# Order of the last token tiles and of the weight splits in a fused window attention and mixture-of-experts kernel

## The chip, the core and the metric

One core of one Trainium2 chip runs the whole kernel. The metric is the device time of one execution in microseconds (us). The engines named below: TensorE (PE, with PEld for its weight loads), VectorE (DVE), ScalarE (ACT), GpSimd (POOL) and SyncE (SP, which issues most of the transfers).

## What is computed

First a causal attention with a window of 64 positions (8 batches, 8 heads, 576 positions, head size 64), all in float32; then a mixture of experts with one expert per token, over the 4608 rows of 512 that the attention gives.

```python
scores = scale * np.matmul(q, k.transpose(0, 1, 3, 2))       # masked to 0 <= rel < 64
attn = softmax(scores)                                       # over the last axis
x = matmul(attn, v).transpose(0, 2, 1, 3).reshape(4608, 512)
do_compute = x @ w_skip > 0
logits = x[do_compute] @ w_gate                              # 8 experts
e_idx, gate_w = argmax(logits), softmax(logits)[e_idx]
h = np.maximum(xc[mask] @ w1[e], 0.0)                        # 512 -> 1024, per expert e
y[mask] = gate_w[mask, None] * (h @ w2[e])                   # 1024 -> 512
out = x.copy(); out[do_compute] = xc + y
```

## The kernel before, in words

**Attention.** The tokens come in 36 tiles of 128 (NT = 36). A loop over t = 0 to 34 is a software pipeline written out by hand: iteration t issues the scores of tile t + 1, the transposes of the finished rows x of an older tile (`transpose_x`), the transposes of the probabilities of tile t (`transpose_p`), the softmax of tile t + 1 (`soften`: maximum on DVE, then eight exponentials on ACT, four of them at once and four when the returned function `softened` is called), the products with v of tile t - 1 (`tile_out`) and the products of x with the gate weights. From tile 32 on the gate logits are computed tile by tile (`logits`): 16 small products, which write into the bank that the transposes of x used, and a copy of the result (`lg`, ACT). In iterations 33 and 34 `its[0].split` also transposes the rows gathered for the first expert item, casts them on ACT (`xh`) and subtracts on DVE (`xl`).

**Order.** Each engine works through its instructions in the order of the program text, within `tc.manual_schedule()`; between engines only semaphores hold. So the order in which the helpers are called is the order of each engine's queue.

**Banks.** The transposes of x and of p, the logits by rows, the x of the first item and the products `p1` of the experts all take turns in two PSUM buffers of one tag, "t". The pool "late" (tags g, u, w) takes the place of the score buffers when the loop is over.

**Routing.** `route` is a generator that works out a group of tiles' places in the experts' lists in small steps on DVE (`gmx`, `gd`, `gfi`, `gfm`, `goh`, `gohb`, later `gds`, `gs`, `gdi`), with one exponential on ACT (`gex`) and small sums on PE; it queues the writes into the lists on POOL (L628). `routes(n)` takes n steps of what stands in `late`. The last group, tiles 30 to 35, is put into `late` by `logits(35)`.

**Experts.** The work is ten items (256, 288, 128, 360, 328, 288, 248, 240, 160 and 104 rows), each in four quarters. A step k does the products up of quarter k (`up`: two halves f0 and f1 of twelve products each into `p1`, then `hh` = relu on ACT and `hl` = the rest on DVE, which frees `p1`) and the products down of quarter k - 2 (`down`). float32 is computed as three products of values split in two, so every weight piece (512 KB, 128 x 1024, two for each quarter) is loaded by SP into one of six buffers `raw` and split by `weight_split`: a cast on ACT (`whi`, L809) and a subtraction on DVE (`wlo`, L810). There are 72 pieces, numbered in order of first use: 0, 1, 2 and 4 are the up weights of item 0's quarters, 3, 5, 7 and 9 its down weights, 6, 8, 10, 12 the up weights of item 1, and so on. The split pieces stand in a ring of ten. The load of piece n + 6 waits for the split of piece n.

**Chunks.** `expert_chunks` yields after each half of `up` and of `down` and at the end of a step. `expert_chunk` first orders weight splits (`weights_to`) and then lets the generator run on to its next yield. How far it splits: `now` is what the current step needs, `need` what the next step needs as well; while `late` is not empty at most one more than before; `short` is set for the call after the first half of a quarter of a two-tile item and ahead of a step of one. Behind the loop the calls are mixed with the last tiles in this order: x of tile 33, one weight split, products of tile 34, logits 33, call 1 (item 0, quarter 0, f0), p of tile 35, x of tile 34, call 2 (f1), products of tile 35, logits 34, calls 3 and 4 (end of step 0; quarter 1, f0), x of tile 35, call 5 (quarter 1, f1), logits 35, the first step of the last route. Then, while `late` is not empty, two steps of the route and a call: call 6 (transposes of the first rows of item 1, end of step 1), call 7 (quarter 2, f0), call 8 (f1), calls 9 and 10 (down of quarter 0) and so on. Call 5 falls into a moment at which `late` is empty.

Of the kernel before, what the change touches and what calls it, by code (L numbers as in the profile page):

```python
# [10 lines left out]
F32 = mybir.dt.float32  # L11
# [11 lines left out]
P = 128  # L23
NB = S // 64
NT = N // P
NDC = D // P
# [35 lines left out]
RATE = 1  # L62
# [90 lines left out]
def window_attention_moe(ctx: ExitStack, tc, a, out):  # L153
# [163 lines left out]
    banks = {}  # L317
# [18 lines left out]

    def transpose_x(t):
        x = xns.pop(t)
        px = psum.tile([P, NDC, P], F32, name="px", tag="t", bufs=2)
        for c in range(NDC):  # L340
            tick(2, nc.tensor.transpose(px[:, c], x[:, c * P : (c + 1) * P], ident))  # L341
        s0, n = BATCH.get(t, (SINGLY, 4))
        if t == s0:
            xts[s0] = xs.tile([P, NDC, 4, P], F32, name="xt4", bufs=1)
        xt = xts[s0][:, :, (t - s0) % 4]
        nc.scalar.copy(xt, px)  # L346
        if t >= SINGLY:
            singles[t] = px, xt
        elif t == s0 + n - 1:
            ready.append(s0)  # L350
# [384 lines left out]
    late = []  # L735
# [31 lines left out]
    ring, used = [], {}  # L767
# [308 lines left out]
    with tc.manual_schedule():  # L1076
# [33 lines left out]
        for t in range(NT - 1):  # L1110
            score(t + 1)
            if t >= 3:
                transpose_x(t - LAG[t])
            masks = transpose_p(t)
            columns = logit_columns(t)
            feed(t, 0)
            softened = soften(t + 1)
            pace(1)
            feed(t, 1)
            if t == 1:  # L1120
                load_constants()
            if t == 5:
                nc.gpsimd.tensor_copy(base, cf[:, off["base"]])
            masks()
            columns()
            if t >= 1:
                summed = tile_out(t - 1)
                rows = logit_rows()
                softened()
                if t >= FIRSTX:  # L1130
                    its[0].split(xhl[0], t - FIRSTX, "t")()
                if t - LAG[t] >= SINGLY:
                    logits(t - LAG[t])
                if t == TURN:
                    transpose_x(t - 2)
                rows()
                summed()
            else:
                softened()
                feed(t, 2)  # L1140
                feed(t, 3)
            routes(1 if t < 15 else 2 if t < 20 else 3)
            pace(1 if t >= TWICE or len(paced) > 4 else 0)
# [12 lines left out]
        def expert_chunk():  # L1156
            k = place[0]
            last = len(steps) - 1
            need = max(when[part(min(k + 1, last), 0)], when[part(min(k - 1, last), 1)] if k else 0) + 1
            now = max(when[part(min(k, last), 0)], when[part(k - 2, 1)] if k >= 2 else 0) + 1  # L1160
            if turning[0]:
                turning[0] = False
                weights_to(now)
            elif late:
                weights_to(max(now, min(need, ptr["split"] + 1)) if ptr["use"] else now)
            elif steps[min(k, last)][0] >= len(its) - 2:
                weights_to(now if short[0] else max(now, min(need + 2, ptr["split"] + 1)))
            else:
                eager = 0 if short[0] or gathered[0] < 3 else min(ptr["split"] + RATE, ptr["free"] + min(RING, len(ring)) - 1)
                weights_to(max(need, eager))  # L1170
            place[0], c = next(chunks)

        transpose_x(NT - 3)
        weight_split(ptr["split"])
        ptr["split"] += 1
        summed = tile_out(NT - 2)
        logits(NT - 3)
        summed()
# [289 lines left out]
```

## Time and profile before

| what | us |
|---|---|
| median of 3 runs | 414.01 |
| lowest and highest | 413.55, 416.78 |
| profiled execution | 408.61 |
| its span, first to last instruction | 407.0 |
| mean granted TensorE clock | 0.997 |
| PE, DVE, ACT, POOL busy | 376.0, 270.8, 224.4, 178.2 |

The busy time of PE counts matmuls whose ends are modelled, so that a busy PE is not PE at its peak. In the listings in order of time an idle time in brackets is that of the engine just before the instruction, with what ended it.

### The profile page before, as it was taken

How to read it: one execution, taken by the hardware profiler on the slowest of the kernel's cores; microseconds unless marked ns; L12 is line 12 of the kernel's file. 1: busy time of each engine (PE TensorE's matmuls, PEld its weight loads, DVE VectorE, ACT ScalarE, POOL GpSimd, SP SyncE). 2: the span in 40 equal slices, each digit the busy share in tenths (PEclk: the TensorE clock that was granted, in tenths of full speed). 3: DMA queues.
4: the chain of work that ended last, by engine and by line, in shares of the span. 5: the costliest groups of instructions: out<-in, count | busy, mean ns of one | idle time of the engine just before them, and what ended most of it. 6: DMA issues, size and time to landing. Idle time of an engine off the chain costs nothing. (4 is left out here: it accounts for less than half of the span.)

```text
span 407.0 us, 13642 instructions
## 1 busy us (share of the span) xinstructions
PE 376.0 (92%) x5425; PEld 318.1 (78%) x5425; DVE 270.8 (67%) x552; ACT 224.4 (55%) x643; POOL 178.2 (44%) x222
## 2 busy tenths in 40 slices
PE   4879898989889997999999999999999999999993
PEld 3667787767676866898788898888889889888872
DVE  2667778868688856797616789764555566764591
ACT  3767787767667865564315646334425344452670
POOL 5545445467767583475262718116106423010121
PEclk9999999999999999999999999999999999999998
DMA  8988889869877798668738866657657776685460
GB/s 271 321 278 272 284 266 316 299 216 289 279 241 215 220 340 294 200 202 297 275 115 276 263 194 204 209 174 235 217 161 249 262 238 188 207 250 174 156 230 28
DMA packets 40677, 95.68 MB, mean 235 GB/s; under 512 B 7216, under 2 KB 9021, under 8 KB 40604
## 3 DMA queue, kind: packets, MB, share of 16 engines
q1 hardware_dynamic: 33124, 78.21, 59.3%
q0 software_dynamic: 4896, 10.02, 7.5%
q10 hardware_dynamic: 2592, 6.57, 4.8%
q8 instruction: 43, 0.70, 0.7%
q14 instruction: 22, 0.18, 0.1%
HBM read 80.57 MB, written 14.91 MB: 235 GB/s over the span
## 5 line engine op out<-in xcount | busy, mean ns | idle before, releaser
L810 DVE TENSOR_TENSOR wlo<-raw,whi 128x1024 fp32r<-128x1024 f32 x72 | 86.5, 1222 | 24.2 <-ACT whi L809 22.2
L917 ACT ACTIVATE hh<-p 128x256 fp32r<-128x256 f32 (+4 forms) x56 | 22.5, 403 | 94.4 <-PE p L862 91.8
L809 ACT CAST whi<-raw 128x1024 fp32r<-128x1024 f32 x72 | 73.7, 1049 | 0.0
L303 POOL TENSOR_TENSOR ptm<-pm,mask 128x512 f32<-128x512 f32 x36 | 45.9, 1275 | 53.8 <-ACT pm L302 53.6
L860 PE MATMUL p<-x,whi 128*128 128x288 f32 (+5 forms) x224 | 67.4, 301 | 1.8 <-DVE hl L920 1.3
L862 PE MATMUL p<-x,wlo 128*128 128x288 f32 (+5 forms) x224 | 66.0, 295 | 0.6 <-DVE wlo L810 0.6
L861 PE MATMUL p<-x,whi 128*128 128x288 f32 (+5 forms) x224 | 65.8, 294 | 0.0
L285 ACT ACTIVATE s<-ps,nmx 128x64 f32<-128x64 f32 x288 | 62.8, 329 | 1.2
L946 POOL DMA_INDIRECT out<-yo,les x15 | 15.4, 1029 | 95.3 <-DVE yo L945 88.0
L444 PE MATMUL av<-vm,ptm 64*64 64x65 f32 x2048 | 47.4, 223 | 9.2 <-issue 9.1
L920 DVE SCALAR_TENSOR_TENSOR hl<-p,hh 128x256 fp32r<-128x256 f32 (+4 forms) x56 | 24.8, 444 | 46.3 <-ACT hh L917 26.8
L444 PEld LDWEIGHTS av<-vm,ptm 64*64 64x64 f32 x2048 | 39.6, 134 | 16.3 <-issue 14.9
L628 POOL DMA_INDIRECT lists<-ent,gdi x36 | 38.3, 1063 | 19.9 <-issue 12.6
L860 PEld LDWEIGHTS p<-x,whi 128*128 128x128 f32 x224 | 42.2, 188 | 4.7 <-DVE hl L920 1.9
L861 PEld LDWEIGHTS p<-x,whi 128*128 128x128 f32 x224 | 42.2, 188 | 0.9
L862 PEld LDWEIGHTS p<-x,wlo 128*128 128x128 f32 x224 | 42.2, 188 | 0.8 <-DVE wlo L810 0.8
L259 PE MATMUL ps<-k,q 64*64 64x128 f32 (+1 forms) x1024 | 38.5, 274 | 0.9 <-DMA q<-qT 0.4
L276 DVE COPY_PREDICATED ps<-sel,ps 128x512 f32<-128x512 int32 x36 | 24.9, 690 | 18.2 <-PE ps L259 14.0
L346 ACT COPY xt<-px 128x512 f32<-128x512 f32 x36 | 21.2, 589 | 23.8 <-PE px L341 17.6
L259 PEld LDWEIGHTS ps<-k,q 64*64 64x64 f32 x1024 | 31.0, 138 | 4.3 <-issue 2.2
L860 PE MATMUL yv<-whi,hh 128*128 128x512 f32 (+1 forms) x72 | 28.8, 400 | 0.0
L862 PE MATMUL yv<-whi,hl 128*128 128x512 f32 (+1 forms) x72 | 28.2, 392 | 0.0
(188 smaller groups left out, 741.7 us busy)
## 6 DMA issues: line engine op xcount, KB each, us to landing
raw<-wq SPq DMA_DIRECT2D x72, 512.0 KB
vm<-vp SPq DMA_DIRECT2D x32, 260.0 KB
q<-qT SPq DMA_DIRECT2D x32, 256.0 KB
out<-x SPq DMA_DIRECT2D x32, 256.0 KB
k<-kT SPq DMA_DIRECT2D x24, 256.0 KB
w<-wq ACTq DMA_DIRECT2D x12, 512.0 KB
k<-kT SPq DMA_DIRECT2D x8, 384.0 KB
kt<-kT SPq DMA_DIRECT2D x8, 256.0 KB
```

Source lines behind the costliest of these rows:

```text
L259: tick(4, nc.tensor.matmul(ps[64 * hf : 64 * hf + 64, z, p, 64 * w.start :], q[h, p], k[h, w, p], start=True, stop=True, skip_group_check= ...
L276: nc.vector.copy_predicated(cur, sel.unsqueeze(1).unsqueeze(1).to_broadcast([P, 2, 4, 64]), ps[..., :64])
L285: nc.scalar.activation(s[:, q, z], cur[:, z, q], AF.Exp, bias=nmx[:, z, q : q + 1], scale=0.125)
L303: nc.gpsimd.tensor_tensor(part(0, 2), split(pm[:, 0:2], 2), kept(2), op=ALU.mult)
L444: ins = tick(4, nc.tensor.matmul(av[64 * hf : 64 * hf + 64, z, q * VW : (q + 1) * VW], ptm[h, q, 2 * hf + 1 - w], win[hf][w][h, q], start= ...
L628: ins = nc.gpsimd.indirect_dma_start(out=lists, out_offset=bass.IndirectOffsetOnAxis(ap=di, axis=0), in_=ent.bitcast(I32), in_offset=None, ...
L809: nc.scalar.copy(hi, raw)
L810: nc.vector.tensor_tensor(lo, raw, hi.bitcast(F32), op=ALU.subtract)
L860: nc.tensor.matmul(o, lh, rh, start=first, stop=False)
L861: nc.tensor.matmul(o, lh, rl, start=False, stop=False)
L862: nc.tensor.matmul(o, ll, rh, start=False, stop=last)
L920: beat(nc.vector.scalar_tensor_tensor(hl[:, f, :m], p1[:, :m], 0.0, hh[:, f, :m].bitcast(F32), op0=ALU.max, op1=ALU.subtract))
```

## The change

Four edits. In the loop's last iteration, t = 34, the second four exponentials of tile 35 are issued behind the split of the gathered x and the logits of tile 32 instead of ahead of them. Behind the loop the first weight split stands ahead of the transposes and the copy of x of tile 33. The transposes of x of tiles 34 and 35 (and the logits in the same bank) use a bank of their own, tag "u" of the pool "late". And `expert_chunk` orders splits by another rule where `late` is empty and the item is not one of the last two: where `short` is set only what the step needs now, elsewhere at most one more than before (`RATE` is 1), up to the ring or, before three items are gathered, up to `need + 2`.

```diff
     def transpose_x(t):
         x = xns.pop(t)
-        px = psum.tile([P, NDC, P], F32, name="px", tag="t", bufs=2)
+        if t < NT - 2:
+            px = psum.tile([P, NDC, P], F32, name="px", tag="t", bufs=2)
+        else:
+            px = banks["late"].tile([P, NDC, P], F32, name="px", tag="u", bufs=1)
         for c in range(NDC):
...
                 rows = logit_rows()
-                softened()
+                if t < NT - 2:
+                    softened()
                 if t >= FIRSTX:
                     its[0].split(xhl[0], t - FIRSTX, "t")()
                 if t - LAG[t] >= SINGLY:
                     logits(t - LAG[t])
+                if t == NT - 2:
+                    softened()
                 if t == TURN:
                     transpose_x(t - 2)
...
             elif steps[min(k, last)][0] >= len(its) - 2:
                 weights_to(now if short[0] else max(now, min(need + 2, ptr["split"] + 1)))
             else:
-                eager = 0 if short[0] or gathered[0] < 3 else min(ptr["split"] + RATE, ptr["free"] + min(RING, len(ring)) - 1)
-                weights_to(max(need, eager))
+                lead = ptr["free"] + min(RING, len(ring)) - 1 if gathered[0] >= 3 else need + 2
+                weights_to(now if short[0] else max(now, min(lead, ptr["split"] + RATE)))
             place[0], c = next(chunks)
 
-        transpose_x(NT - 3)
         weight_split(ptr["split"])
         ptr["split"] += 1
+        transpose_x(NT - 3)
         summed = tile_out(NT - 2)
```

## Rows read from the trace of the kernel before

**Rows 1.** The page: busy time of PE, and PE in 40 slices (tenths).

```profile
PE 376.0 (92%) x5425; PEld 318.1 (78%) x5425; DVE 270.8 (67%) x552; ACT 224.4 (55%) x643; POOL 178.2 (44%) x222
...
PE   4879898989889997999999999999999999999993
```

**Rows 2.** Table by stretch: length, busy time (instructions) per engine, clock, DMA.

```profile
180.00:200.00 20.00, 18.73 (x115) 16.65 (x114) 16.54 (x34) 11.07 (x20) 9.23 (x9) 1.00 0.79 272
...
240.00:260.00 20.00, 20.00 (x113) 17.95 (x112) 17.47 (x39) 8.93 (x14) 9.47 (x12) 1.00 0.69 223
```

**Rows 3.** Groups by line: the weight split (busy us, mean ns, idle before).

```profile
L810 DVE TENSOR_TENSOR wlo<-raw,whi 128x1024 fp32r<-128x1024 f32 x72 | 86.5, 1222 | 24.2 <-ACT whi L809 22.2 <-issue 1.6
L809 ACT CAST whi<-raw 128x1024 fp32r<-128x1024 f32 x72 | 73.7, 1049 | 0.0
```

**Rows 4.** In order of time, PE, 156 to 174 us (start, us, instruction).

```profile
156.59 0.66 PE L341 MATMUL px<-ident,x 128*128 128x128 f32 x4 [1.05 <-ACT lg L418]
...
158.48 0.64 PE L414 MATMUL px<-wg,xt 128*64 128x9 f32 x16
...
160.12 0.39 PE L862 MATMUL p<-x,wlo 128*128 128x256 f32 x1 [0.57 <-DVE wlo L810]
...
162.52 0.66 PE L341 MATMUL px<-ident,x 128*128 128x128 f32 x4 [0.49 <-DVE hl L920]
...
169.14 0.39 PE L860 MATMUL p<-x,whi 128*128 128x256 f32 x1 [0.49 <-issue]
...
171.79 0.39 PE L860 MATMUL p<-x,whi 128*128 128x256 f32 x1
...
173.34 0.60 PE L849 MATMUL px<-ident,xg 128*128 128x128 f32 x4
```

**Rows 5.** In order of time, ACT, 154 to 174 us.

```profile
154.20 1.75 ACT L285 ACTIVATE s<-ps,nmx 128x64 f32<-128x64 f32 x8
...
157.76 1.05 ACT L809 CAST whi<-raw 128x1024 fp32r<-128x1024 f32 x1
...
169.16 2.00 ACT L809 CAST whi<-raw 128x1024 fp32r<-128x1024 f32 x2
...
173.33 0.25 ACT L505 ACTIVATE gex<-gd 128x48 f32<-128x48 f32 x1 [1.59 <-DVE gd L497]
```

**Rows 6.** In order of time, DVE, 158 to 173 us.

```profile
158.84 1.23 DVE L810 TENSOR_TENSOR wlo<-raw,whi 128x1024 fp32r<-128x1024 f32 x1 [1.70 <-ACT whi L809]
...
172.86 0.19 DVE L495 TENSOR_REDUCE gmx<-lg 128x6 f32<-128x48 f32 x1
```

**Rows 7.** In order of time, PE, 190 to 198 us: products up of item 1.

```profile
190.28 0.29 PE L860 MATMUL p<-x,whi 128*128 128x288 f32 x1
...
192.41 0.40 PE L860 MATMUL p<-x,whi 128*128 128x288 f32 x1 [0.39 <-DVE hl L920]
...
197.88 0.40 PE L860 MATMUL p<-x,whi 128*128 128x288 f32 x1 [0.88 <-DVE hl L920]
```

**Rows 8.** In order of time, DVE and ACT, 179 to 198 us.

```profile
179.63 0.17 DVE L542 TENSOR_REDUCE gdi<-gds 128x6 int32<-128x54 f32 x1
...
188.55 0.38 ACT L917 ACTIVATE hh<-p 128x256 fp32r<-128x256 f32 x1 [3.69 <-PE p L862]
...
191.78 3.90 ACT L809 CAST whi<-raw 128x1024 fp32r<-128x1024 f32 x4
...
192.86 4.63 DVE L810 TENSOR_TENSOR wlo<-raw,whi 128x1024 fp32r<-128x1024 f32 x4 [0.51 <-ACT whi L809]
...
197.41 0.75 DVE L920 SCALAR_TENSOR_TENSOR hl<-p,hh 128x256 fp32r<-128x256 f32 x2
```

**Rows 9.** In order of time, POOL: a list write, and the gather for item 2.

```profile
173.22 0.99 POOL L628 DMA_INDIRECT lists<-ent,gdi  x1 [1.69 <-DVE gmx L495]
...
202.24 1.07 POOL L654 DMA_INDIRECT xg<-out,les  x1 [0.94 <-DMA raw<-wq]
```

**Rows 10.** Table by stretch: behind the last matmul.

```profile
402.00:407.00 5.00, 0.00 (x0) 0.00 (x0) 0.00 (x0) 0.00 (x0) 1.02 (x1) 0.77 0.15 40
```

## What is predicted

> **What bounds the kernel now.** I read the page first: TensorE (PE) is busy for 376.0 of 407.0 us, and its slices show nine tenths or more from about 170 us to the end [rows 1]. The table by stretch then says where time is left: in 180 to 200 us PE lacks 1.27 us of 20, in 240 to 260 nothing [rows 2]. So a change pays only by taking waits off PE between 154 and 206 us, and what PE gains there it keeps, because after it one matmul follows the other to the end. Then I read the three listings in order of time for that stretch, PE first (where does it stand still, and for whom), then ScalarE (ACT) and VectorE (DVE) for the work in front of what it waits for [rows 4 to 8]. In them the reader should see that the waits on PE come from the *order* in ACT and DVE, which work strictly in program order here, and not from how much work they have. One weight split is a cast of 1.05 us on ACT and then a subtraction of 1.22 us on DVE [rows 3], so a matmul that needs a freshly ordered split waits up to 2.3 us. In a row of four, one cast follows the other after 0.95 us and one subtraction after 1.14 us ([rows 8]; (3.90 - 1.05)/3 and (4.63 - 1.22)/3).
>
> **Change 1 to 3: the last token tiles.** In the iteration t = 34 eight exponentials start at 154.20 and take 1.75 us, that is one every 0.197 us; the cast of the gathered x stands behind them, and then the copy of tile 32's logits (`lg`). PE's transposes of x for tile 33 wait 1.05 us for that copy, to 156.59, since they reuse its bank [rows 4]. With four exponentials moved behind, the cast starts at about 155.0, when its transposes are done, and `lg` at 155.62: the transposes start at 155.84, 0.75 earlier. The four exponentials then run from 155.72 (their reader, the transposes of p of tile 35, comes only behind the first chunk's products of 160.12 [rows 4]), so the next ACT work starts at 156.51. It is now the weight split's cast (before: 157.76 [rows 5]); x's copy stands behind it, from 157.46 to 158.05. The logits of tile 33, at 158.48 before [rows 4], wait for that copy and start at 158.08: 0.40 earlier, not 0.75. The rest of the cast's 0.95 us in front of the copy is covered by the products of tile 34, which PE has to do in between anyway.
>
> The subtraction starts at 157.59 instead of 158.84 [rows 6] and ends at 158.82. The first chunk's third matmul, which before waited until 160.12 [rows 4], goes on at about 159.0: 1.1 to 1.2 us earlier. Next the bank: the transposes of x of tile 34 waited 0.49 us for the chunk's `hl` [rows 4]. In a bank of their own they follow the transposes of p at once, and the second chunk's products find a free buffer behind them. That adds 0.6, so the second chunk starts 1.8 us earlier. The same thing at tile 35: there the first products behind the transposes stood still for 0.49 us, at 169.14 [rows 4], for the last chunk's `hl`. So the chunk of 169.14 starts at about 166.8. Sum: **minus 2.35 us**. From below: if the steps behind the first chunk find another wait (GpSimd's masks for tile 35's products), only its 1.2 stays. Nothing can be lost below zero here, since the one thing put in front, the cast, is already charged to the copy. I take 2.35, with 1.2 to 2.4 as bounds: each later gain is a wait that a row shows, with no other due behind it.
>
> **Change 4: one split per chunk.** I counted both rules through all calls of `expert_chunk`. They order the 72 splits alike except in calls 5 to 22. Before: call 5 orders splits 2 and 3; 8 and 9 order 4 and 5; 13 orders 6 and 7; 16 to 22 order 8 to 14, one each. After: 5 none, since the flag `short` is set there and the rule is `now`; 6, 7, 8 and 9 order 2, 3, 4, 5; 11 orders 6; 14 to 21 order 7 to 14; 13 and 22 none. The rows of before agree with the count: two casts in one at 169.16 [rows 5], four in one at 191.78 [rows 8].
>
> *What it costs.* Piece 2 is first used in call 7, by the products that start at 171.79 [rows 4]. Before, its split was done by 171.5. After, call 6 orders it, and ahead of call 6 the program has logits of tile 35, their copy, and the first steps of the last route: `gmx`, `gd` on DVE and the exponential `gex` on ACT, which stood idle 1.59 us for `gd` [rows 5, 6]. So the cast now waits for that chain. Counted from the start T of call 5's products: logits copied at T + 2.47, `gd` at T + 2.75 and `gex` at T + 3.0 (the spacing of `gmx` and `gex`, 0.47 [rows 5, 6]), cast from T + 3.15 to T + 4.20, subtraction from T + 4.23 to T + 5.45. Unhindered the products would start at T + 2.65. They start at T + 4.25, and the third, the first that reads `wlo`, at T + 5.50. Ten more follow at 0.12 us; the transposes that came at 173.34, T + 4.20, [rows 4] now come at T + 6.81. **Plus 2.6 us.** Bounds: 1.6 if only the cast were waited for, and 3.8 if another subtraction of 1.22 [rows 3] got in between. With T = 166.8 that place falls at 173.6, against 173.34: the two parts cancel, to plus 0.25.
>
> *What it moves.* From there both kernels stand alike, but splits 6 and 11 to 14 are ordered one or two calls earlier. Before, PE waited twice for `hl`, which frees the buffer of the products: at 192.41 and at 197.88 [rows 7]. The rows give 0.39 and 0.88 us of idle; with about 0.15 each until the pipeline is full again that is some 1.6 us. The second wait is the row of four: the `hl` at 197.41 stood behind four subtractions that took 4.63 us [rows 8]. Laid end to end in the new order, with the small steps of the expert order in between as before, from 179.85, behind the route's last step [rows 8], DVE does wlo 6 to 181.0, 7 to 185.3, 8 to 187.0, 9 to 188.2, 10 to 189.35, `hl`, 11 to 190.85, `hl`, 12 to 14 to 194.7, and the `hl` that PE needs by 196.5 comes at 195.1. Even if the activations come as late as the one of 188.55 (2.4 us after its last matmul [rows 8], for a reason that the trace doesn't show), it is 196.4. So about 1.4 of the 1.6 us goes: **minus 1.4**, bounds 0 and 1.6.
>
> *Its transfers.* A split issues none itself, but each frees the buffer for the load of the piece six further on, in SP's queue. Loads 8 and 9 start about 1 and 1.4 us later, 12 about 1.9 earlier, 13 one later, 14 as before. No cast stood idle before [rows 3], and casts 8 and 9 come 10 us after their loads begin: I cost it at nothing. Its cover is that lead; for 13 and 14 it is small, and a cast that waits there lands in the bounds above. GpSimd's list writes, held at 173.22 by DVE's `gmx` [rows 9], start some 3.5 us earlier, since no subtraction stands ahead of `gmx` any more; so the gather of the next item's rows at 202.24 [rows 9], which waits for all of them, comes earlier too and will not take the gain back.
>
> **Sum.** Minus 2.35, plus 2.6, minus 1.4: minus 1.15 us. The profiled execution took 408.61 us around a span of 407.0, so I expect 407.45 and 405.85 there. It stands 5.4 us below the median of the runs, 414.01; the difference carried over gives **412.9 us**.
>
> **Rivals.**
> *The fresh split hides.* If ACT or PE did something else in that time, the first part stays whole: minus 2.35, minus 1.4, so 410.3 us. For it: only about 1.6 us of the wait is certain order. Against: the cast stands behind `gex` in an engine that works in order.
> *Nothing is paid back.* If the waits at 192 and 197 hang on the late activations and the loads and not on the row of four, the sum is plus 0.25: 414.3 us. For it: the late activation of 188.55 [rows 8]. Against: four subtractions alone make the second wait.
> *The wait moves in front of the older `hl`* (the slower side). wlo 10 now stands ahead of the `hl` that frees the buffer for the products of 190.28 [rows 7]. That `hl` is due at 189.7 by the order above, the products at 190.5: DVE has 0.85 us to spare. If it runs later than that, each such place costs up to one subtraction, 1.22 us [rows 3], instead of a gain: 414.01 + 0.25 + 1.22 = 415.5 us.
> *The clock falls.* The granted clock was 1.00 (2.4 GHz) in 180 to 200 and 240 to 260 [rows 2] and fell, to a mean of 0.77, behind the last matmul, where PE did nothing any more [rows 10]. If the new stop took it to 1.2 GHz, the 12 matmuls behind it, 1.55 us, would take that again: 412.9 + 1.55 = 414.45 us. The Trainium skill ("TensorE: Matmul & The Clock Gate", section "Why this matters for your kernels") speaks against such stops, and advises against long idle gaps between bursts of matmuls, which drop the clock to half; the trace agrees as far as its end goes. My stop is two pieces of about 1.6 and 1.0 us, with matmuls between.
>
> **How the numbers follow.** Chances: forecast 0.50, split hides 0.16, nothing paid back 0.19, wait moves 0.12, clock 0.03. The range runs from a little under the first rival's 410.3 to a little past the slow one's 415.5: 410.0 to 415.8, which also takes in 3.8 for the stop; what is left out is part of "hides" and some of "moves". One per cent is 4.1 us, about what a measurement here can tell (the three runs lie 3.2 us apart). Under 409.9 only "hides" reaches, with about half its chance and a little from the spread of the runs: 0.10. Over 418.1 none reaches but by several misses: 0.06. Within: 0.84.
>
> **What would show it.** In the profile after: transposes of tile 33 at about 155.8; no wait for `hl` ahead of those of 34 and 35; call 5's products at 166.8. Then, the test of the step that decides, a stop of about 1.6 us for `whi` and one of about 1.0 for `wlo` in the products of piece 2, and the next transposes at 173.6. The four casts in one are gone, and PE waits less than 0.5 us in 190 to 198. If the stop at piece 2 is missing, or is 4 us long, or the waits at 192 and 197 are as before, the matching term was wrong.

## The result and the profile after

| what | before | after |
|---|---|---|
| median of 22 runs each, us | 412.41 | 415.67 |
| lowest and highest, us | 407.86, 416.80 | 411.41, 418.77 |
| profiled execution, us (its span) | 408.61 (407.0) | 416.00 (414.2) |
| mean granted TensorE clock in it | 0.997 | 0.988 |
| PE busy, us | 376.0 | 375.7 |

The ratio of after to before is 1.0073, with an interval of 1.0045 to 1.0102: about 3.0 us slower. That is under 1%, but it is clear of no change, and on the other side than the forecast (1.15 us faster). That the median of after, 415.67, still falls inside the range given (410.0 to 415.8) is luck: the range was laid around 414.01, the median of the first three runs of before. The ratios here leave out executions more than 1.5% above the fastest of their kernel, which the medians keep in, so two variants are compared below by their ratios.

The page of after shows the same work, and a PE that dips where before had nines [rows 1]:

```profile
PE 375.7 (91%) x5425; PEld 319.9 (77%) x5425; DVE 271.5 (66%) x552; ACT 225.0 (54%) x643; POOL 180.6 (44%) x222
...
PE   4879897898989787799989999999999999999993
```

The table by stretch says where PE's time and its clock went (length, busy time and count of PE, PEld, DVE, ACT, POOL, then the clock, the DMA share and GB/s):

```profile
170.00:180.00 10.00, 6.95 (x53) 6.26 (x53) 5.32 (x13) 4.49 (x10) 6.75 (x9) 0.76 0.40 119
...
180.00:200.00 20.00, 20.00 (x129) 18.38 (x128) 17.02 (x42) 12.03 (x20) 10.94 (x8) 0.95 0.75 244
...
200.00:220.00 20.00, 18.42 (x138) 16.17 (x137) 6.82 (x11) 4.43 (x15) 8.32 (x15) 1.00 0.51 176
```

Three microseconds are missing in 170 to 180 us, at a mean clock of 0.76; the records of the granted clock give 1.2 GHz from 175.3 to 182.1 us. The stretch 180 to 200, where before lacked 1.27 us [rows 2], is full. And 1.58 us are missing again in 200 to 220, where before had no wait on PE. PE in order of time shows all three:

```profile
159.72 0.66 PE L344 MATMUL px<-ident,x 128*128 128x128 f32 x4 [1.00 <-ACT lg L421]
...
164.51 0.60 PE L344 MATMUL px<-ident,x 128*128 128x128 f32 x4
...
170.06 0.60 PE L344 MATMUL px<-ident,x 128*128 128x128 f32 x4
170.41 0.36 PE L863 MATMUL p<-x,whi 128*128 128x256 f32 x1
...
172.02 0.64 PE L417 MATMUL px<-wg,xt 128*64 128x9 f32 x16
172.59 0.66 PE L852 MATMUL px<-ident,xg 128*128 128x128 f32 x4
175.79 0.58 PE L863 MATMUL p<-x,whi 128*128 128x256 f32 x1 [2.55 <-ACT whi L812]
...
177.10 0.58 PE L865 MATMUL p<-x,wlo 128*128 128x256 f32 x1 [0.51 <-issue]
177.48 0.41 PE L863 MATMUL p<-x,whi 128*128 128x256 f32 x1
177.69 0.41 PE L864 MATMUL p<-x,whi 128*128 128x256 f32 x1
...
212.72 0.66 PE L852 MATMUL px<-ident,xg 128*128 128x128 f32 x4 [1.58 <-DMA xg<-out,les]
```

The `hl` waits ahead of the transposes of tile 34 and behind those of tile 35 [rows 4] are gone. Piece 2's products wait 2.55 us for `whi`, and from there they come every 0.21 us, not every 0.12. At the first rows of item 2 there is a new wait, for the gather `xg`; before, these transposes started at 205.75 with no wait (shown further below). What stands ahead of piece 2's cast, ACT and then DVE in order of time (with the route's last step `gdi`):

```profile
172.13 0.38 ACT L920 ACTIVATE hh<-p 128x256 fp32r<-128x256 f32 x1 [0.85 <-issue]
173.89 0.17 ACT L421 COPY lg<-px 128x9 f32<-128x9 f32 x1 [1.38 <-PE px L852]
174.56 0.24 ACT L508 ACTIVATE gex<-gd 128x48 f32<-128x48 f32 x1 [0.51 <-DVE gd L500]
174.71 1.03 ACT L812 CAST whi<-raw 128x1024 fp32r<-128x1024 f32 x1
```

```profile
174.09 0.20 DVE L498 TENSOR_REDUCE gmx<-lg 128x6 f32<-128x48 f32 x1 [1.12 <-ACT lg L421]
...
175.78 1.27 DVE L813 TENSOR_TENSOR wlo<-raw,whi 128x1024 fp32r<-128x1024 f32 x1 [0.28 <-ACT whi L812]
...
186.33 0.17 DVE L545 TENSOR_REDUCE gdi<-gds 128x6 int32<-128x54 f32 x1
```

The chain is the one foretold (logits' copy, `gmx`, `gd`, `gex`, cast, subtraction), but the copy came late: 1.23 us behind the last of the logits' products (172.02 + 0.64), with ACT idle. Its row names PE as what ended that wait: in the kept trace the update of PE's semaphore that frees the copy stands at 173.86. So it was PE's release that came late, and not ACT. GpSimd, for the gather (list writes, then the gather of item 2's rows):

```profile
181.21 1.84 POOL L631 DMA_INDIRECT lists<-ent,gdi  x1 [0.30 <-issue]
...
187.26 1.21 POOL L631 DMA_INDIRECT lists<-ent,gdi  x1 [4.21 <-issue]
...
195.01 1.96 POOL L631 DMA_INDIRECT lists<-ent,gdi  x1 [0.30 <-issue]
...
209.21 1.07 POOL L657 DMA_INDIRECT xg<-out,les  x1 [0.94 <-DMA raw<-wq]
```

The last six list writes (187.26 the first, 195.01 the last) wait for the route's last step `gdi`, at 186.33 (179.63 before [rows 8]): GpSimd stands idle 4.21 us ahead of them. The gather comes at 209.21 instead of 202.24 [rows 9]. The same places in before, PE (logits of tile 35, item 2's transposes), ACT (their copy) and GpSimd (first and last of the six writes):

```profile
170.77 0.64 PE L414 MATMUL px<-wg,xt 128*64 128x9 f32 x16
...
205.75 0.66 PE L849 MATMUL px<-ident,xg 128*128 128x128 f32 x4
```

```profile
171.57 0.17 ACT L418 COPY lg<-px 128x9 f32<-128x9 f32 x1
```

```profile
182.31 1.59 POOL L628 DMA_INDIRECT lists<-ent,gdi  x1 [0.30 <-issue]
...
189.78 0.97 POOL L628 DMA_INDIRECT lists<-ent,gdi  x1 [0.30 <-issue]
```

There the six writes came one behind the other after the eight before them, with no wait for `gdi`, and the last stood at 189.78.

**Where the time went.** Executions differ by several microseconds in the attention, so I compare distances from one event to the next: the maximum of tile 35 (ACT `nmx`, 153.96 before), the activations `hh` of call 5 (171.06), of item 0, quarter 3, f0 (180.43), of item 1, quarter 2, f0 (199.76), and the `hh` at 243.21, behind item 2. Each column is the distance less that of before; minus is faster. The last column lists the stretches at 1.2 GHz between 150 and 215 us, by the clock's records of that one execution. Two things limit the comparison. There is one profile of before only, while the sets ran on their own (their medians of before lie between 406 and 413 us), so the columns can hold more than the edit. And in before two casts stand ahead of call 5's `hh`: it starts 1.92 us behind T, the start of call 5's products, and 1.72 behind it in after; counted to T, the last tiles give -1.92 in after and -2.50 in after_here, and the stop 0.2 less, +6.00 and +2.52.

| kernel | last tiles | stop for piece 2 | items 0, 1 | item 2's entrance | sum | 1.2 GHz, us |
|---|---|---|---|---|---|---|
| after | -2.12 | +6.20 | -1.78 | +1.54 | +3.84 | 175.3 to 182.1 |
| after_here | -2.70 | +2.72 | -1.72 | +0.29 | -1.41 | none |
| late2 | -2.85 | +4.11 | -1.78 | -0.52 | -1.04 | 168.8 to 172.3 |
| fill20 | -2.84 | +2.72 | -1.54 | +0.46 | -1.20 | none |
| fill_late2 | -2.32 | +2.72 | -1.78 | -0.82 | -2.20 | none |
| rule_alone | +0.26 | +2.72 | -1.78 | +1.57 | +2.77 | 154.9 to 158.3 |
| call5_two | -0.26 | 0.00 | -0.83 | +3.51 | +2.42 | 157.4 to 160.8, 208.6 to 212.0 |
| call5_late2 | -1.39 | 0.00 | -1.78 | +2.05 | -1.12 | none |
| banks_order | +2.43 | -0.02 | -0.62 | +0.05 | +1.84 | 151.7 to 162.0 |
| banks_late2 | -1.90 | +0.01 | -0.70 | -1.03 | -3.62 | none |
| banks_late2_b | -1.23 | 0.00 | -0.93 | +0.37 | -1.79 | none |
| stop_only | +0.37 | +6.07 | -0.80 | +0.52 | +6.16 | 159.2 to 166.1, 176.3 to 183.1 |
| stop_fill | -1.12 | +3.86 | -1.04 | +1.36 | +3.06 | 159.0 to 162.4 |
| edit1_back | -1.06 | +6.31 | -1.79 | +1.08 | +4.54 | 155.8 to 159.3, 172.9 to 179.7 |
| behind5 | +1.41 | +2.19 | -0.69 | +1.74 | +4.65 | 157.3 to 167.5 |
| behind5_late2 | -2.05 | +2.19 | -1.78 | +1.84 | +0.20 | none |
| ahead_route | -2.20 | +5.54 | -1.79 | +1.46 | +3.01 | 173.9 to 180.7 |

### The profile page after: what moved, and what is told of

Same layout as the page of the kernel before. It is cut to its first block, busy times and chain, and to the rows that moved or that the text cites. A ratio compares the mean times of both kernels' runs of the same rounds, so it can differ in the third digit from the quotient of the medians.

```text
span 414.2 us, 13645 instructions
## 1 busy us (share of the span) xinstructions
PE 375.7 (91%) x5425; PEld 319.9 (77%) x5425; DVE 271.5 (66%) x552; ACT 225.0 (54%) x643; POOL 180.6 (44%) x222
## 5 line engine op out<-in xcount | busy, mean ns | idle before, releaser
L863 PE MATMUL p<-x,whi 128*128 128x288 f32 (+5 forms) x224 | 68.2, 304 | 2.6 <-ACT whi L812 2.5
L865 PE MATMUL p<-x,wlo 128*128 128x288 f32 (+5 forms) x224 | 66.9, 299 | 0.5 <-issue 0.5
L864 PE MATMUL p<-x,whi 128*128 128x288 f32 (+5 forms) x224 | 66.7, 298 | 0.0
L447 PE MATMUL av<-vm,ptm 64*64 64x65 f32 x2048 | 46.5, 223 | 11.7 <-issue 11.7
L631 POOL DMA_INDIRECT lists<-ent,gdi x36 | 39.3, 1092 | 22.4 <-issue 16.0
L863 PEld LDWEIGHTS p<-x,whi 128*128 128x128 f32 x224 | 43.2, 193 | 4.9 <-ACT whi L812 2.8
L864 PEld LDWEIGHTS p<-x,whi 128*128 128x128 f32 x224 | 43.2, 193 | 0.9
L865 PEld LDWEIGHTS p<-x,wlo 128*128 128x128 f32 x224 | 43.1, 193 | 0.8 <-issue 0.8
```

The costliest lines, as they stand in the source:

```text
L447: ins = tick(4, nc.tensor.matmul(av[64 * hf : 64 * hf + 64, z, q * VW : (q + 1) * VW], ptm[h, q, 2 * hf + 1 - w], win[hf][w][h, q], start= ...
L631: ins = nc.gpsimd.indirect_dma_start(out=lists, out_offset=bass.IndirectOffsetOnAxis(ap=di, axis=0), in_=ent.bitcast(I32), in_offset=None, ...
L863: nc.tensor.matmul(o, lh, rh, start=first, stop=False)
L864: nc.tensor.matmul(o, lh, rl, start=False, stop=False)
L865: nc.tensor.matmul(o, ll, rh, start=False, stop=last)
```

## The experiments

Each set has its own runs of the kernel before, with these medians and mean clocks: set 1, 407.87 us and 0.990; set 2, 406.19 and 0.989; set 3, 412.74 and 0.990 (two far outlying executions left out of the clock); set 4, 413.15 and 0.988. Clocks below are means over the executions of a kernel.

### Set 1: the edits apart

**banks_order**: edits 1 to 3 alone, the splits by the old rule.

```diff
-                lead = ptr["free"] + min(RING, len(ring)) - 1 if gathered[0] >= 3 else need + 2
-                weights_to(now if short[0] else max(now, min(lead, ptr["split"] + RATE)))
+                eager = 0 if short[0] or gathered[0] < 3 else min(ptr["split"] + RATE, ptr["free"] + min(RING, len(ring)) - 1)
+                weights_to(max(need, eager))
```

> The changed kernel with the old rule for the splits: only the edits of the last token tiles. Theory A (the loss comes from the new rule: in call 5 no split is ordered, PE stops about 3 us for piece 2, and the clock falls to 1.2 GHz behind the stop): no stop in front of the products of piece 2, one granted clock of 1.00 from 10 us to the last matmul, the products of call 5 about 2 us earlier than before counted from the last iteration, and a time about 2 us below the kernel before, 0.995 of it. Theory B (the bank and the order of the last tiles cost, or the loss is chance in the attention part): no faster than before, 1.000 to 1.007.

406.71 us, ratio 0.9986 (0.9937 to 1.0036), clock 0.988. There is no stop for piece 2. The gain of the last tiles is missing in the profiled execution, whose clock was low in just that place; banks_late2 below shows it.

**rule_alone**: the kernel before with the new rule alone (the same diff the other way round).

> The kernel before with the new rule for the splits alone. Theory A: the stop for piece 2 as in the changed kernel (2.5 us for whi, 0.5 for wlo), the clock at 1.2 GHz for some 7 us behind it, and 5 to 6 us above the kernel before, 1.013 of it, since the gain of the other edits is missing. Theory B: within 0.3 per cent of the kernel before.

409.97 us, ratio 1.0065 (1.0017 to 1.0112), clock 0.986. The rule brings the stop (+2.72), with no low stretch behind it in this execution, gives back 1.78 and loses 1.57 of that at item 2's gather.

**call5_two**: the change, but call 5 orders splits 2 and 3 as before.

```diff
-                weights_to(now if short[0] else max(now, min(lead, ptr["split"] + RATE)))
+                weights_to(need if ptr["split"] == 2 else now if short[0] else max(now, min(lead, ptr["split"] + RATE)))
```

> The changed kernel, but in call 5 the splits 2 and 3 are ordered as before; everywhere else the new rule stands. Theory A: no stop, no fall of the clock, the waits for hl at item 1 gone too, but the gather for item 2 limits: 2 us below the kernel before, 0.995. If the gather does not limit, the waits at item 1 pay as well: 3.5 us below, 0.9915. Theory B: as the changed kernel, 1.005 to 1.01.

409.58 us, ratio 1.0075 (1.0029 to 1.0120), clock 0.985. The stop is gone, the loss is not: so the stop alone is not the cause. PE in order of time, in an execution of 412.87 us, the highest of its twelve:

```profile
207.95 0.66 PE L852 MATMUL px<-ident,xg 128*128 128x128 f32 x4 [2.55 <-DMA xg<-out,les]
...
208.58 0.42 PE L864 MATMUL p<-x,whi 128*128 128x288 f32 x1
208.80 0.44 PE L865 MATMUL p<-x,wlo 128*128 128x288 f32 x1
209.04 0.44 PE L863 MATMUL p<-x,whi 128*128 128x288 f32 x1
```

PE waits 2.55 us for the gather, and then the products come at 0.24 us instead of 0.13: the clock fell behind this wait as it did behind the stop in the profile of after.

**fill20**: the change, with 20 transposes of the identity, used by nothing, between calls 6 and 7.

```diff
             expert_chunk()
+            if fills:
+                fills = 0
+                fl = banks["late"].tile([P, NDC, P], F32, name="fl", tag="w", bufs=2)
+                for c in range(20):
+                    nc.tensor.transpose(fl[:, c % NDC], ident, ident)
```

> The changed kernel with 20 transposes of the identity, into a bank that nothing reads, between call 6 and call 7, that is in PE's stop ahead of piece 2 (about 2.2 us of work, 0.11 us each, more than the kernel needs). If the clock costs beside the wait: the granted clock stays at 1.00, and the time lies some 3 us below the changed kernel, about 1.001 of the kernel before. If only the wait costs: no better than the changed kernel, 1.007, or 0.2 us worse.

406.00 us, ratio 0.9997 (0.9955 to 1.0039), clock 0.991, the highest of the set. The stop is still there (+2.72); with the extra work on PE the change is no slower than before. The change without filler did not run in this set, so what the filler is worth is read from set 3.

### Set 2: the gather of item 2

**after_here**: the change itself.

> The changed kernel itself, beside its variants on one chip, with the granted clock of every execution. Theory C (clock): the work outside the low stretches is as long as before, and what is lost is lost in stretches at 1.2 GHz; so time minus (1 - mean clock) x time lies within 1 us of the same figure of the kernel before (403.6 there in the last set), while the mean clock is 0.004 to 0.008 below it, and the time 2 to 4 us above it. Theory W (waits): the mean clock is the same within 0.002 and the waits for piece 2 and for item 2's rows make the 3 us; then the figure without the clock's loss is itself 2 to 3 us above before.

407.46 us, ratio 1.0048 (1.0006 to 1.0091), clock 0.988 against 0.989. Here neither theory holds as written: the clock is hardly lower, and the time without the clock's loss (402.4 us) lies 0.3 us above before's 402.1. But its profiled execution, at 403.43 us the fastest of its twelve, ran with the clock up and shows the change as it was forecast: -2.70, +2.72, -1.72, +0.29. The stop in it, PE and then ACT in order of time:

```profile
163.86 0.64 PE L417 MATMUL px<-wg,xt 128*64 128x9 f32 x16
...
166.45 0.39 PE L863 MATMUL p<-x,whi 128*128 128x256 f32 x1 [1.37 <-ACT whi L812]
...
167.71 0.39 PE L865 MATMUL p<-x,wlo 128*128 128x256 f32 x1 [0.76 <-DVE wlo L813]
```

```profile
164.55 0.17 ACT L421 COPY lg<-px 128x9 f32<-128x9 f32 x1 [0.20 <-PE px L417]
```

Two pieces, 1.37 and 0.76 us, and the logits' copy on time, where after had 2.55 and a copy 1.2 us late.

**late2**: the change, with item 2's transposes one half of a quarter later.

```diff
-    SPLITS = {1: ((3, 0),), 2: ((2, 1), (3, 0)), 3: ((1, 1), (2, 1), (3, 0))}
+    SPLITS = {1: ((3, 1),), 2: ((2, 1), (3, 0)), 3: ((1, 1), (2, 1), (3, 0))}
```

> The changed kernel, with the transposes of item 2's rows one half of a quarter later. Theory G (the gather limits): the payback of items 0 and 1 was eaten by the wait for that gather, 1.46 us in the profiled execution of the change, 2.4 to 2.6 in others; without it the kernel is 1.5 to 3 us faster than the changed kernel beside it, PE shows no wait ahead of item 2's transposes, and the mean clock rises by 0.001 to 0.003, since one place at which the clock falls is gone. Rival: another wait takes its place (the cast or the subtraction of item 2's rows is then needed at once), and the time is within 0.7 us of the changed kernel.

405.72 us, ratio 1.0014 (0.9974 to 1.0055): 1.4 us under after_here by the ratios, whose intervals overlap; the mean clock did not rise (0.988). The wait is gone from PE:

```profile
203.91 0.66 PE L852 MATMUL px<-ident,xg 128*128 128x128 f32 x4
```

**fill_late2**: both, filler and later transposes.

> The changed kernel with the 20 filler transposes between calls 6 and 7 and with item 2's transposes one half later. Theory C: both places at which PE stands still for 1.5 us or more in the experts' part are covered or gone, so the mean clock is at or above before's (0.990 or more), and the time is 1.5 to 3 us under the kernel before (ratio 0.993 to 0.996). Theory W: the stop for piece 2 is still there, covered only by filler, so the ratio stays at 1.000 to 1.004.

405.78 us, ratio 0.9989 (0.9947 to 1.0030), clock 0.990. The ratio is lower than after_here's, with intervals that overlap; beside late2 the filler added nothing that can be told here.

**banks_late2**: edits 1 to 3 and the later transposes, with the old rule.

> The kernel before with the edits of the last token tiles (no new rule for the splits), and item 2's transposes one half later. banks_order showed a wait of 0.58 us for that gather and a ratio of 0.9986. Theory C: 0.6 us of wait less and perhaps one fall of the clock less: ratio 0.994 to 0.998. Rival (the wait for item 2 is no limit where the old rule holds): the same 0.998 to 1.000.

404.13 us, ratio 1.0003 (0.9961 to 1.0045), clock 0.989: not to be told from before. Its profile keeps 1.90 us of the last tiles.

### Set 3: the stop by itself

**stop_only**: the new rule for splits 2 to 5, the old one from there on.

```diff
+                eager = 0 if short[0] or gathered[0] < 3 else min(ptr["split"] + RATE, lead)
+                if ptr["split"] >= 6:
+                    weights_to(max(need, eager))
+                else:
-                weights_to(now if short[0] else max(now, min(lead, ptr["split"] + RATE)))
+                    weights_to(now if short[0] else max(now, min(lead, ptr["split"] + RATE)))
```

> The changed kernel with the new rule only for splits 2 to 5 and the old one from there on: the stop for piece 2 and the last tiles' edits, without the payback in items 0 and 1. Theory (terms as measured so far): last tiles -2.3 to -2.8, stop +2.7, payback none, gather 0 to +0.5, so -0.3 to +0.6 us while the clock stays up; with a fall of the clock at the stop in about half of the executions (+1.4 to +3.5 in each) +0.5 to +2.2 us on the mean. PE's wait for hl near 192 and 197 is back. Rival (no payback exists, and the stop alone is what the change does): the same time as the changed kernel, and the waits for hl stay away.

416.41 us, ratio 1.0059 (1.0014 to 1.0105), clock 0.981: no execution is above 0.988. One wait for `hl` is back, and of the 1.78 us in items 0 and 1 only 0.80 are left:

```profile
205.54 0.40 PE L863 MATMUL p<-x,whi 128*128 128x288 f32 x1 [0.72 <-DVE hl L923]
```

**stop_fill**: the same with the 20 filler transposes.

> The same as stop_only, with the 20 filler transposes of the identity between calls 6 and 7, which keep PE busy in the wait for piece 2's split and are used by nothing. Theory C (the wait brings falls of the clock with it): no low stretch within 10 us behind the filler, mean clock 0.002 to 0.004 above that of stop_only, and 0.8 to 1.7 us faster than it. Rival (falls come at chance places, the stop has no part in them): the same clock within 0.001 and the same time within 0.5 us.

413.92 us, ratio 1.0038 (1.0005 to 1.0071), clock 0.992. By the ratios 0.9 us faster than stop_only, which the intervals do not settle, with more work on PE and the copy as late; the mean clock is clearly higher (0.992 against 0.981). The table by stretch for both, 170 to 180 us (stop_only, then stop_fill), and then PE in stop_fill:

```profile
170.00:180.00 10.00, 6.94 (x57) 6.25 (x58) 6.40 (x18) 4.25 (x9) 5.74 (x8) 0.82 0.32 90
```

```profile
170.00:180.00 10.00, 8.92 (x86) 8.32 (x85) 6.14 (x16) 5.11 (x10) 6.84 (x7) 1.00 0.37 114
```

```profile
173.60 2.35 PE L1382 MATMUL fl<-ident 128*128 128x128 f32 x20
176.27 0.39 PE L863 MATMUL p<-x,whi 128*128 128x256 f32 x1 [0.32 <-issue]
...
177.53 0.39 PE L865 MATMUL p<-x,wlo 128*128 128x256 f32 x1 [0.76 <-DVE wlo L813]
```

The wait for piece 2 is as long, but filled; the clock stays at 1.00 and the stop costs 3.86 us instead of 6.07. This pair is the plainest evidence here: the wait itself is one price, and the clock that falls with it another, of 2.2 us between these two executions (6.07 less 3.86).

**call5_late2**: call5_two with item 2's transposes later.

> The changed kernel, but call 5 orders splits 2 and 3 as before (no stop for piece 2), and item 2's transposes come one half later (no wait for that gather). Theory G (the stop and the gather wait are what took the gain; the clock adds to it by chance): from the maximum of tile 35 on it keeps the last tiles' 2.3 to 2.8 us and the 1.7 us of items 0 and 1, less what call 5 pays for its two casts (up to 1), so 3 to 4.5 us under the kernel before, ratio 0.989 to 0.994. Rival: call5_two alone was 1.0075, with a mean clock 0.005 below before's; if that comes from falls of the clock in other places than the item-2 wait, this kernel stays at 1.000 or above.

411.58 us, ratio 0.9996 (0.9954 to 1.0038), clock 0.990 like before's, where call5_two stood 0.005 below its own. The clock is back, but the 3 to 4.5 us did not come: the wait for the gather is shorter (0.74 us, 2.55 in call5_two) but not gone, and two other waits at item 2's entrance came to it. PE in order of time, then ACT, first here, then in late2:

```profile
206.62 0.66 PE L852 MATMUL px<-ident,xg 128*128 128x128 f32 x4 [0.74 <-DMA xg<-out,les]
...
215.81 0.44 PE L938 MATMUL pt<-ident,hs 128*128 128x128 f32 x2 [0.42 <-ACT hs L933]
...
218.34 0.66 PE L852 MATMUL px<-ident,xg 128*128 128x128 f32 x4 [0.67 <-DVE hl L940]
```

```profile
211.01 3.23 ACTq L803 DMA_DIRECT2D w<-wq  x2
215.38 0.38 ACT L933 ACTIVATE hs<-p 128x256 f32<-128x256 f32 x1 [7.47 <-remote]
```

```profile
207.94 0.92 ACTq L803 DMA_DIRECT2D w<-wq  x2
209.97 0.38 ACT L933 ACTIVATE hs<-p 128x256 f32<-128x256 f32 x1 [4.79 <-PE p L865]
```

Item 2's first activation `hs` stands in ACT's queue behind two transfers, whose issue spans 3.23 us here and 0.92 in late2. Before had 2.56 at this place, without a wait on PE. What holds the second transfer is not in the trace.

**edit1_back**: the change with the exponentials in front again.

```diff
-                if t < NT - 2:
-                    softened()
+                softened()
...
-                if t == NT - 2:
-                    softened()
```

> The changed kernel with the second four exponentials of tile 35 in front again. By the prediction's step the copy of tile 32's logits then starts 0.75 us later against the maximum of tile 35 (2.41 us behind it as in the kernel before, against 1.62 to 1.77 in undisturbed executions with the edit), and the first chunk's activation about 0.4 to 0.8 us later. Rival (that copy waits for a late release by PE, as in the profiled execution of the change, where it came 2.35 behind): the same distance with and without the edit, and no difference in time.

414.45 us, ratio 1.0057 (1.0015 to 1.0099). The copy of tile 32's logits comes 2.29 us behind the maximum of tile 35; with the edit it is 2.13 to 2.33 in the same set. So in this set the rival holds and the edit moved nothing; in set 2 the same distance was 1.62 to 1.77 in three of four kernels with the edit.

### Set 4: the stop made shorter

**behind5**: piece 2's split right behind call 5; call 6 orders none.

```diff
+        held6 = [1]
...
+            elif late and held6:
+                held6.pop()
+                weights_to(now)
...
         expert_chunk()
+        weights_to(ptr["split"] + 1)
         logits(NT - 1)
         routes(1)
```

> The changed kernel, with piece 2's split ordered right behind call 5 instead of in call 6: ahead of the copy of tile 35's logits and of the last route's first steps. Theory (order makes the stop, its length makes the clock fall): the cast runs while PE does the logits; a wait of 0.2 us for whi and 0.8 for wlo is left instead of 2.7 to 3.9; no low stretch there; mean clock 0.004 to 0.008 above that of the changed kernel, and 1.5 to 4 us faster than it (ratio to the kernel before 0.994 to 1.000, the wait for item 2's rows of 0.5 to 1.5 us included). Rival: the logits' copy and the route, now 1.05 us later, hold the lists and so the gather of item 2, and the gain ends there: 1.002 to 1.005.

415.99 us, ratio 1.0031 (0.9986 to 1.0077), clock 0.983. PE's waits at piece 2 are down to 0.25 and 0.76 us (the whole distance still loses 2.19) and no low stretch follows, but in the profiled execution the clock fell for 10.2 us in the last tiles, and the mean clock is as low as with the stop. This kernel speaks against the stop as the only place of the falls.

**behind5_late2**: the same with item 2's transposes later.

> The same, with the transposes of item 2's rows one half later. Theory: last tiles -2.3 to -2.8, stop +0.5 to +1.2, items 0 and 1 -1.7, no wait for the gather: 2.5 to 3.5 us under the kernel before, ratio 0.991 to 0.995. Rival (another wait at item 2's entrance takes its place, as ACT's transfers of the quarter-filled tile's weights did in the kernel with call 5's old rule): 0.997 to 1.000.

412.72 us, ratio 1.0010 (0.9975 to 1.0045), clock 0.989. By the ratios it is 0.9 us faster than behind5, with intervals that overlap. At item 2's entrance both profiles lose the same (+1.74, +1.84): PE still waits 0.95 us for the gather here (1.42 in behind5), and ACT's transfers span 3.26 us, so on the waits the rival is right. What rose is the mean clock, by 0.006; that this makes the difference is argued, not shown.

**ahead_route**: the split behind the logits' copy, ahead of the route's steps; call 6 orders none, by the same lines as in behind5 (not shown again).

```diff
         expert_chunk()
         logits(NT - 1)
+        weights_to(ptr["split"] + 1)
         routes(1)
```

> The changed kernel, with piece 2's split behind the copy of tile 35's logits and ahead of the last route's steps: the stop is shorter by the wait for gd and by gex, about 0.8 us, so 1.9 us, or 3.1 where the logits' copy is late. Theory (the length decides): with 1.9 us the clock does not fall there, with 3.1 it falls in some executions only; mean clock between that of behind5 and of the changed kernel, time 0.8 to 3 us under the changed kernel's. Rival (any stop there brings the fall): mean clock as in the changed kernel (0.983 where the kernel before has 0.990), and only the 0.8 us gained.

415.04 us, ratio 1.0055 (1.0018 to 1.0092), clock 0.985. PE in order of time:

```profile
174.11 0.58 PE L863 MATMUL p<-x,whi 128*128 128x256 f32 x1 [1.76 <-ACT whi L812]
...
175.37 0.58 PE L865 MATMUL p<-x,wlo 128*128 128x256 f32 x1 [0.46 <-DVE wlo L813]
175.74 0.42 PE L863 MATMUL p<-x,whi 128*128 128x256 f32 x1
175.96 0.41 PE L864 MATMUL p<-x,whi 128*128 128x256 f32 x1
```

The wait is 0.8 us shorter, as expected, and the clock fell all the same (products every 0.21 us), and on the mean (0.985) it stands near the changed kernel's 0.983. That the length of the wait decides the fall is not borne out.

**banks_late2_b**: banks_late2 beside the others.

> The kernel before with the last tiles' edits, the old rule for the splits, and item 2's transposes one half later, beside behind5_late2 on one chip. Theory: the last tiles' 1.9 to 2.8 us and some of items 0 and 1 (0.7), no stop: ratio 0.993 to 0.997, and 0.5 to 1 us slower than behind5_late2. Rival (the last tiles' gain is lost to falls of the clock there, as in three profiles of other variants): 0.998 to 1.001.

411.04 us, ratio 0.9979 (0.9951 to 1.0008), clock 0.991. It has the lowest ratio of its set; that it beats the kernel before is not shown, since the interval takes in 1.

Over all sets, the three kernels with the old rule (banks_order, banks_late2, banks_late2_b) have ratios of 0.9979 to 1.0003. The eight with all or part of the new rule, no filler and item 2's transposes in their old place have 1.0031 to 1.0075. So the loss comes with the rule; where it arises is read from the profiles.

## Why the prediction was wrong

The forecast was -1.15 us; the profile of after has +3.84 from the maximum of tile 35 to the `hh` behind item 2, and the runs +3.0. The steps that failed are the size of the stop, the clock that was priced at nothing in the sum, and the gather that was said not to take the gain back.

1. *Last tiles, -2.35*: right. -2.12 in after, -2.3 to -2.85 in the four executions of sets 1 and 2 that have the four edits. Within it, "`lg` 0.75 earlier" did not happen in after: PE still waits 1.00 us for it at 159.72, against 1.05 [rows 4], because the copy itself came late. The other steps (no wait ahead of tile 34's transposes or behind tile 35's) came as told.
2. *The count of splits and the place of the stop*: right. Call 6 orders piece 2, behind the logits' copy and `gex`.
3. *The stop, +2.6*: the term that failed, by its size. In after_here, fill20, fill_late2 and rule_alone it is 2.72. In after, and in the kernels of sets 3 and 4 that have the stop with the split behind the copy, the logits' copy comes 1.1 to 1.2 us later: it starts at T + 3.48 in after (T = 170.41), and at T + 2.30 in after_here, which ends it at the T + 2.47 that was told. I took that distance from before, where the copy stands behind two casts and came 0.16 us behind the products. In set 3 it came 0.14 behind them in call5_late2, which has these casts, and 1.17 to 1.22 in the three kernels without; so the casts seem to have hidden the delay. The prediction had an upper bound of 3.8; stop_fill, with the late copy and the clock up, has 3.86.
4. *The clock*: the second failed step, a rival with 0.03. It fell at the stop in after, late2, stop_only, edit1_back and ahead_route, five of the seven profiles that have it unfilled, and in none of the three with filler. Where it fell it cost 1.4 us (late2, 4.11 less 2.72) to 2.3 (after, 6.20 less 3.86): more than the 1.55 foreseen in the long case, since it outlasted the 12 products and took in those of the next half. The Trainium skill ("TensorE: Matmul & The Clock Gate", section "Why this matters for your kernels") warns of idle gaps between bursts of matmuls that send the clock to half; the trace agrees with it at this stop (0.76 in 170 to 180 us), though the page names longer gaps than the 2.55 us here. I had named the rule and gave it almost no chance, on the ground that the stop is two pieces with products between. But in four of the five the clock fell inside the first piece, ahead of those products (at 175.3 in after, where the products start at 175.79; at 173.9 in ahead_route, in a wait of 1.76 us that ended at 174.11).
5. *Payback, -1.4*: right in its mechanism and a little past its bound of 1.6: -1.72 to -1.79 in after and in eight others, and the waits at 192 and 198 are gone. But stop_only gets 0.80 with the old rule from split 6 on, so about 1.0 belongs to the rule there.
6. *"The gather comes earlier and will not take the gain back"*: failed. I looked at the list writes behind `gmx`, which do come earlier, counted from the maximum of tile 35 (17.3 us behind it in after, 19.3 in before); the last six now wait for `gdi`, which hangs on the same stop. In before they did not: they queued behind the earlier writes, and the last stood at 189.78, in after at 195.01. The gather then came at 209.21, and item 2's transposes 3.51 us behind it, as in before. So a gain of items 0 and 1 alone runs into this gather: +1.54 in after, +1.57 in rule_alone; late2, where the transposes come later, has -0.52.
7. *Transfers, nothing*: right in effect. Casts stood idle 2.7 us in all, 2.5 of it behind DVE, and no wait on PE is put down to these loads.

The terms that differ account for it: the late copy with the clock +3.6 (6.20 less 2.6), the gather +1.5, the last tiles +0.2, payback -0.4, together +5.0 on -1.15, which is the +3.84. Of the rivals, "the wait moves" (415.5 us) lies nearest to the measured median, but by luck: no wait for an older `hl` shows in after between 183 and 212 us. The filler pair shows the clock's part at the stop, the later transposes the gather's. What stays open: why PE's release of the copy is late in some sets; why the clock falls in the last tiles, in seven profiles of kernels with and without the stop; and in set 2, how much of the 1.9 us is the clock's, since its mean hardly moved there.

## What to carry to other kernels

When a split or any other producer is moved behind a longer chain, price the wait from the latest arrival of each link, not from where another wait has hidden it, and price the clock as a second term wherever PE would stand still in dense work. Ask which gather or load follows from the moment that is pushed later: a gain ahead of it counts only as far as that transfer moves too. Where the wait can't be avoided, idle transposes on PE can be cheaper than silence, here by 2.2 us of 6.07 between two profiled executions; over the runs the ratios (1.0059 and 1.0038) lie too close to tell.

## What the runs showed of the hardware

Within one kernel the mean clock of an execution went from 0.968 to 0.998 (before, set 4), so a profile of one execution can't price an effect of this size: before's own profile, at 0.997, was one of the good ones. The stretches at 1.2 GHz in the table above were 3.4, 6.8 or 10.2 us long. And the copy of the logits, behind 16 small products, started 0.05 us behind the last of them in after_here (163.86 + 0.64, 164.55) and 1.23 us behind it in after, with the same instructions around it; where no cast stands ahead of it, sets 1 and 2 agree with the one, sets 3 and 4 with the other. PE's update that frees it stands at 164.52 in after_here and at 173.86 in after, so it is PE's release that is late.
